# Batches 1 to 3 of a block-sparse attention: three terms of softmax times values summed in one set of PSUM columns

## The chip, the cores and the metric

One core of one Trainium2 chip runs the whole program. The metric is the device time of one execution in microseconds (us); the kernel before took 771.23 us (median of three runs, 769.91 to 771.23). The engines are named as in the profile: PE is the matrix engine and PEld its weight loads, DVE is VectorE, ACT ScalarE, POOL GpSimd, and SP the queue that issues most of the DMAs.

## The reference

The input is q, k and v of 4 batches, 8 heads, 768 rows and 64 columns, and three random block numbers for each of 24 blocks of 32 rows. A row block sees its neighbours, the first and the last block, and its three sampled blocks; the first and the last row block see everything. The result goes through a gated feed-forward layer.

```python
scores = scale * np.matmul(q, k.transpose(0, 1, 3, 2))
scores = np.where(mask, scores, -1000000000.0)
attn = np.exp(scores - np.max(scores, axis=-1, keepdims=True))
attn = attn / (np.sum(attn, axis=-1, keepdims=True) + 1e-09)
x = np.matmul(attn, v)                  # heads side by side: 3072 x 512
g, val = x @ w_gate, x @ w_val          # 512 x 1536 each
out = (g * (1.0 / (1.0 + np.exp(-g))) * val) @ w_out
```

## The kernel before

The 3072 rows are cut into 24 tiles of 128 rows (4 row blocks of 32), and these into 9 chunks: three of two tiles (batch 0), then six of three tiles. Each chunk passes through attention and then through the feed-forward layer. From chunk 3 on, and in the feed-forward part of chunk 2, numbers that need more than 16 bits are kept as two fp16 parts, high and low, and a product is the sum of three: high times high, high times low, low times high.

**A row block in batches 1 to 3** is the function `block`; there are 66 of them, worked on in 33 pairs. Its 256 keys are gathered into `kring` and its 256 values into a part of `w2all` (high and low parts side by side, `vg`). `scores` makes the scores on PE (L1157), `top` masks them and takes the maxima on DVE (L1171), `power` exponentiates on ACT (L1189), `high` (ACT, L410) and `low` (DVE, L413) split the result into `pp`, and a DMA transposes `pp` into `pts`. `product` (L1224) multiplies `pts` by the values into a PSUM bank `pv` that the two blocks of a pair share. When both are there, `x_sum` (L1240, DVE) adds the two column parts of each result, from PSUM into SBUF (the space of `pts` is used again), `x_scale` (L1243, DVE) multiplies by the reciprocals `rr` of the softmax sums, `x_turn` (L1249, PE) transposes into the first half of the `pv` bank, and `x_put` writes the feed-forward input `xall` (ACT L1519, DVE L1520).

In `product` four row tiles u stand in four column strips of PE, 32 columns each, and work side by side; four matmuls, one for each strip, are called a quad here. For each of two head groups g there are four quads: the high weights multiply 128 columns (high and low values, `w_ = 2`), the low weights 64 (high values, `w_ = 1`). So a block has 32 matmuls, half of them of 128 columns and half of 64, and 512 columns of a bank hold a pair: 4 results of 64 columns, each in two parts.

**Batch 0** has a form of its own, `pair0`, in fp32: `product` (L1448), then `scaled` (L1456, DVE), which multiplies a PSUM tile of 128 x 256 by `rr`, then a transposition (L1465). Full rows have `full_rows` (L940, L1011). The feed-forward part is `ffn_in` (L1743 in fp32 for chunks 0 and 1, L1749 in fp16 from chunk 2 on; DVE L1758 and L1763; POOL L1771) and `ffn_out` (L1812). The weights come as fp64 and are decoded on DVE by three passes for each pair of rows (L450, L451, L452), up to about 140 us, then split into halves (L410, L413).

**What sets the order.** Every step is a task of one engine, added by `add` with its needs and buffers. `Plan.order` emits the tasks in the order of the list `TURN`, written out by hand: 2750 numbers. Each engine runs its own instructions in that order. The estimates in the calls of `add` (such as `PV_US`) are not read when the program is built; `TURN` alone decides. PSUM has rings of two banks for `qk`, two for `pv` and four for `ffn`.

Of the kernel before, what the change touches and what calls it, by code (L numbers as in the profile page):

```python
# [13 lines left out]
ALU = mybir.AluOpType  # L14
AX = mybir.AxisListType

P = 128
B, H, S, D = 4, 8, 768, 64
BLK = 32
# [16 lines left out]
PV_US = 0.47  # L36
# [154 lines left out]
]  # L191


# [1717 lines left out]
```

## Time and profile before

| | us |
|---|---|
| three timed runs: median (lowest, highest) | 771.23 (769.91, 771.23) |
| the profiled execution | 768.49 |
| its span, first to last instruction | 766.7 |
| PE busy / DVE busy / ACT busy / POOL busy | 736.3 / 568.3 / 481.9 / 239.1 |
| PE without work from 200 to 690 us | 8.1 |

The profiled execution is 2.74 us (0.36%) shorter than the median; outside its span lie 1.8 us. "Busy" of PE counts a matmul from its start to its modelled end, so matmuls that overlap count once. A number behind "x" is a count of instructions. Idle time in brackets is that of the engine just before the row, with what ended it.

### The profile page before, as it was taken

Reading aid. Unit: us, or ns where it says so; the run is one execution under the profiler, and the core shown is the slowest. Engines: PE = TensorE matmul, PEld = TensorE weight load, DVE = VectorE, ACT = ScalarE, POOL = GpSimd, SP = SyncE. Lnnn points to the kernel's source line nnn. Section 1 sums busy time; section 2 is a strip of 40 time slices with the busy share of each in tenths; the row PEclk is TensorE's granted clock in tenths of the full one; section 3 lists DMA queues with packets and bytes.
Section 4 is the critical chain, followed back from the end, with each engine's and each line's share of the span. In section 5 each row is a group of like instructions: output and inputs, shape, how many; then the busy total and the mean of one; then the engine's idle time right before and its main releaser. Section 6 shows DMA issues by size and latency. Waiting matters only on the chain.

```text
span 766.7 us, 22166 instructions
## 1 busy us (share of the span) xinstructions
PE 736.3 (96%) x8793; PEld 467.1 (61%) x8793; DVE 568.3 (74%) x1581; ACT 481.9 (63%) x1117; POOL 239.1 (31%) x290
## 2 busy tenths in 40 slices
PE   4899999999999999999999999999999999999998
PEld 3576888764686556545655465545665566555655
DVE  6999999998899997537999777656977766733220
ACT  4999745886986875855968665755856553443221
POOL 4887012213154322321233232202333332202120
PEclk9999999999999999999999999999999999999999
DMA  8756576467686987887687996886686656350001
GB/s 282 251 182 211 188 239 250 150 209 166 127 180 176 211 159 139 209 266 189 148 195 153 231 187 176 174 168 148 149 144 124 190 109 146 73 98 15 1 1 42
DMA packets 156472, 123.75 MB, mean 161 GB/s; under 512 B 113456, under 2 KB 124080, under 8 KB 156368
## 3 DMA queue, kind: packets, MB, share of 16 engines
q1 hardware_dynamic: 150736, 105.03, 56.5%
q0 software_dynamic: 5632, 17.31, 8.4%
q8 instruction: 69, 1.13, 0.6%
q14 instruction: 35, 0.29, 0.1%
HBM read 84.55 MB, written 11.01 MB: 125 GB/s over the span
## 4 chain that ended last, share of the span: by engine, by line
PE 58%; DVE 26%; ACT 6%; issue 5%; DMA 2%; POOL 1%; DVEq 1%; SPq 0%; POOLq 0%; ACTq 0%
PE p L1749 29%; PE po L1812 20%; PE qk L1157 2%; PE pv L1224 2%; DVE act L1758 2%; DVE act L1763 2%; DVE w1t L413 1%; DMA ptsf<-ppf 1%; DVE pp L413 1%; DVE e L1171 1%; DVE w1t L451 1%; DVE pts L1240 1%; DVE kring L1135 1%; DVE w2all L451 1%; DVE pts L1243 1%
## 5 line engine op out<-in xcount | busy, mean ns | idle before, releaser
L1749 PE MATMUL p<-xall,w1t 128*128 128x384 f16 (+1 forms) x2016 | 323.2, 319 | 1.0 <-DVE act L1758 1.0
L1749 PEld LDWEIGHTS <-w1t 128*128 128x128 f16 x2016 | 194.3, 98 | 115.9 <-issue 4.7
L1771 POOL TENSOR_TENSOR h<-act,h 128x384 f16<-128x384 f32 (+1 forms) x108 | 101.5, 942 | 341.5 <-ACT h L1768 336.6
L1812 PE MATMUL po<-w2all,h 128*128 128x512 f16 (+1 forms) x900 | 191.9, 371 | 0.0
L1812 PEld LDWEIGHTS <-h 128*128 128x128 f16 x900 | 86.6, 98 | 94.4 <-issue 1.9
L1145 POOL DMA_INDIRECT w2all<-vd,vidx x66 | 65.7, 996 | 85.9 <-PE pv L1224 61.7
L1743 PE MATMUL p<-xall,w1t 128*128 128x256 f32 x384 | 87.8, 383 | 1.8 <-DVE act L1758 1.6
L1758 DVE SCALAR_TENSOR_TENSOR act<-act,p 128x384 f32<-128x384 f32 (+1 forms) x108 | 54.0, 503 | 45.9 <-ACT act L1754 43.7
L1768 ACT CAST h<-act 128x384 f16<-128x384 f32 (+1 forms) x108 | 50.5, 471 | 55.5 <-DVE act L1763 55.2
L1754 ACT ACTIVATE act<-p,gsc 128x384 f32<-128x384 f32 (+1 forms) x84 | 47.0, 559 | 53.5 <-PE p L1749 37.5
L1743 PEld LDWEIGHTS p<-xall,w1t 128*128 128x128 f32 x384 | 71.0, 190 | 14.5 <-DVE act L1758 3.1
L1189 ACT ACTIVATE e<-e,nb,es 128x256 f32<-128x256 f32 x132 | 78.2, 593 | 2.2
L413 DVE SCALAR_TENSOR_TENSOR pp<-e,pp 128x512 f16<-128x512 f32 x66 | 49.2, 751 | 14.2 <-ACT pp L410 13.4
L1763 DVE SCALAR_TENSOR_TENSOR act<-act,hs,p 128x384 f32<-128x384 f32 (+1 forms) x84 | 49.4, 590 | 8.8 <-PE p L1749 5.7
L1171 DVE CUSTOM_DVE_ANT_1 e<-qk,msk 128x256 f32<-128x256 f32 x132 | 49.6, 416 | 3.9 <-PE qk L1157 3.4
L410 ACT ACTIVATE pp<-e 128x512 f16<-128x512 f32 x66 | 40.4, 622 | 0.7
L1687 POOL TENSOR_TENSOR sqx<-sqx 128x768 bf16<-128x768 bf16 (+3 forms) x18 | 21.6, 1202 | 60.8 <-ACT sqx L1683 46.6
L1644 ACT ACTIVATE ot<-po,oc 128x512 f32<-128x512 f32 (+1 forms) x25 | 16.6, 664 | 37.6 <-PE po L1812 32.1
L1135 DVE COPY kring<-kst 128x256 f16 x198 | 37.5, 244 | 1.5 <-DMA kst<-stage 0.9
L1157 PE MATMUL qk<-kring,qs 128*32 128x256 f16 x1056 | 35.7, 273 | 0.4
L1186 ACT ACTIVATE nb<-mx,es 128x2 f32<-128x2 f32 x66 | 19.1, 290 | 25.8 <-DVE mx L1171 25.8
L1224 PEld LDWEIGHTS <-pts 128*32 128x32 f16 x2112 | 25.5, 97 | 9.5 <-issue 8.3
(200 smaller groups left out, 980.3 us busy)
## 6 DMA issues: line engine op xcount, KB each, us to landing
stage<-in_w_dram SPq DMA_DIRECT2D x36, 512.0 KB, 5.1
w2all<-vd SPq DMA_DIRECT2D x66, 192.0 KB, 4.1
qraw<-in_q_dram SPq DMA_DIRECT2D x18, 512.0 KB, 4.9
out_dram<-ot SPq DMA_DIRECT2D x19, 256.0 KB, 4.0
qn<-in_q_dram SPq DMA_DIRECT2D x36, 128.0 KB, 3.5
stage<-in_v_dram SPq DMA_DIRECT2D x9, 512.0 KB, 5.6
vd<-stage SPq DMA_DIRECT2D x9, 512.0 KB, 2.8
stage<-in_k_dram SPq DMA_DIRECT2D x9, 512.0 KB, 5.7
```

The source lines that it names most:

```text
L413: nc.vector.scalar_tensor_tensor(lo, src, scale, hi, op0=ALU.mult, op1=ALU.subtract)
L1145: nc.gpsimd.indirect_dma_start(vf[0:96, 1, :], None, bt.vd, bass.IndirectOffsetOnAxis(ap=vidx[0:96, qb : qb + 1], axis=0))
L1157: nc.tensor.matmul(stv[u * BLK : (u + 1) * BLK, g].rearrange("p s k -> p (s k)"), o.q[:, l, u, g, col : col + BLK], kg[:, 2 * u + g].rearr ...
L1171: nc.vector.tensor_tensor_reduce(ev[:, g], stv[:, g], o.g.msk[:, qb, :].unsqueeze(2).broadcast_to([P, 8, BLK]), scale=1.0, scalar=-3.0e38, ...
L1189: nc.scalar.activation(ev[:, g], ev[:, g], AF.Exp, bias=nb_[:, g : g + 1], scale=o.g.es[:, 0:1], accum_out=both["rs"][:, n % 2, g : g + 1],)
L1743: nc.tensor.matmul(t[:, 0:tc_], w[:, i + 1, k_ * P : (k_ + 1) * P], x_k(k_), start=k_ == 0, stop=k_ == NKT - 1)
L1749: nc.tensor.matmul(t[:, 0:tc_], w_[:, f, m, k_, :], x_k(k_, l), start=i == 0, stop=i == 11)
L1758: nc.vector.scalar_tensor_tensor(a_, a_, 1.0, pg.tile[:, 0:tc_], op0=ALU.add, op1=ALU.mult)
L1763: nc.vector.scalar_tensor_tensor(a_, a_, sc, pw.tile[:, 0:tc_], op0=ALU.mult, op1=ALU.mult)
L1768: nc.scalar.copy(hv(f)[:, 0, :], act.tile[:, 0:tc_])
L1771: nc.gpsimd.tensor_tensor(hv(f)[:, 1, :], act.tile[:, 0:tc_], hv(f)[:, 0, :], op=ALU.subtract)
L1812: nc.tensor.matmul(po.tile[:, cs], hv(f)[:, l, ts_], w2h[:, f, m, cs], start=f == 0 and i == 0, stop=f == NF - 1 and i == 2)
```

## The change

In `product` of batches 1 to 3 all three terms go into the same 64 columns: for each group g six quads of 64 columns (for each half cc of the keys: high by high, high by low, low by high) take the place of two of 128 and two of 64. So a block has 48 matmuls and 48 weight loads where it had 32 and 32, over as many columns in all (12 quads of 64 for 4 of 128 and 4 of 64). A pair fills 256 columns of the bank instead of 512. `x_sum` is gone, and `x_scale` reads PSUM where it read SBUF. `TURN` is a new list of 2717 numbers, 33 fewer. DMA work is as before.

```diff
-PV_US = 0.47
+PV_US = 0.48
...
 TURN = [
-    0, 60, 2, 1, 5, 7, 6, 22, 21, 29, 28, 3, 36, 38, 4, 8, 23, 42, 10, 9, 84, 220, 18, 40, 11, 30, 16, 129, 19, 14,
+    0, 60, 2, 1, 5, 7, 6, 22, 21, 29, 28, 3, 36, 38, 4, 8, 42, 23, 10, 9, 84, 220, 18, 40, 16, 11, 129, 17, 19, 30,
...
-            to = pv.tile.rearrange("p (b g l d) -> p b g l d", b=2, g=2, l=2)[:, n % 2]
+            to = pv.tile[:, 0:256].rearrange("p (b g d) -> p b g d", b=2, g=2)[:, n % 2]
 
             for g in range(2):
-                for i, (cc, l) in enumerate(((0, 0), (0, 1), (1, 1), (1, 0))):
+                for i, (cc, l, m) in enumerate((cc, l, m) for cc in range(2) for l, m in ((0, 0), (0, 1), (1, 0))):
                     for u in range(4):
-                        rows_, w_ = slice(u * BLK, (u + 1) * BLK), 1 if l else 2
                         nc.tensor.matmul(
-                            to[rows_, g, 0:w_],
+                            to[u * BLK : (u + 1) * BLK, g],
                             pq[:, g, l, cc, u],
-                            vg[:, cc, 0:w_, 2 * u + g, :],
+                            vg[:, cc, m, 2 * u + g, :],
                             start=i == 0,
-                            stop=i == 3,
+                            stop=i == 5,
                             tile_position=(0, u * BLK),
                         )
...
-        def x_sum():
-            two = pv.tile.rearrange("p (n l d) -> p n l d", l=2, d=D)
-            nc.vector.tensor_reduce(xs(), two.rearrange("p n l d -> p n d l"), axis=AX.X, op=ALU.add)
-
         def x_scale():
             nc.vector.tensor_tensor(
-                xs(), xs(), both["rr"].rearrange("p b g -> p (b g)").unsqueeze(2).broadcast_to([P, 4, D]), op=ALU.mult
+                xs(), pv.tile[:, 0:256].rearrange("p (n d) -> p n d", d=D), both["rr"].rearrange("p b g -> p (b g)").unsqueeze(2).broadcast_to([P, 4, D]), op=ALU.mult
             )
...
-            a = add("DVE", 0.6, x_sum, [a], rank, use=[pv, pts])
-            a = add("DVE", 0.33, x_scale, [a, both["inv"]], rank, use=[pts])
+            a = add("DVE", 0.34, x_scale, [a, both["inv"]], rank, use=[pv, pts])
             a = add("PE", 0.25, x_turn, [a, t_id], rank, use=[pv, pts])
```

The new list leaves the first 83 tasks of PE, the first 121 of DVE and the first 107 of ACT where they were, which reaches to about 90 us; behind that, tasks of all engines stand earlier or later by a few places. Line numbers of the kernel after are 2 to 8 lower. Two places follow.

The first is PE between 103 and 149 us, the time in which it multiplies chunks 0 and 1 by the fp32 weights (`p`, L1743 before, L1735 after). `xs_21` is the last result of chunk 2, the first input of the fp16 feed-forward part, and the row that reads it is its transposition. Before:

```order
L1743 MATMUL p_11_2273<-xall,w1t 128x256 x4
L1743 MATMUL p_11_2291<-xall,w1t 128x256 x4
L1743 MATMUL p_7_2301<-xall,w1t 128x256 x4
L1465 MATMUL pv_21_2013<-ident,xs_21_2287 128x128 x2
L407 LDWEIGHTS ones_h
L407 MATMUL nrm_v_2319<-vacc_2289,ones_h 128x3
L1743 MATMUL p_7_2322<-xall,w1t 128x256 x4
```

After:

```order
L1735 MATMUL p_2_2030<-xall,w1t 128x256 x4
L1735 MATMUL p_2_2050<-xall,w1t 128x256 x4
L1735 MATMUL p_3_2062<-xall,w1t 128x256 x4
L1457 MATMUL pv_21_1974<-ident,xs_21_2067 128x128 x2
L1735 MATMUL p_3_2073<-xall,w1t 128x256 x4
L1735 MATMUL p_4_2085<-xall,w1t 128x256 x4
```

The transposition stood behind 39 of the 48 `p` products of chunks 0 and 1, and now stands behind 21 of them.

DVE makes `xs_21` for it (L1456 before, L1448 after). The same place on DVE, before:

```order
L1574 TENSOR_TENSOR rsf_1_1_1739<-rsf_1_1_1739 128x1
L1575 TENSOR_SCALAR rsf_1_1_1739<-rsf_1_1_1739,vs_921 128x1
L1576 RECIPROCAL rsf_1_1_1739<-rsf_1_1_1739 128x1
L1456 TENSOR_TENSOR xs_21_2287<-pv_21_2013,rr_21_1889 128x256
L413 SCALAR_TENSOR_TENSOR w2all<-w2all,oss 128x512
```

After:

```order
L448 TENSOR_SCALAR w1t<-stage 128x1024
L449 SCALAR_TENSOR_TENSOR w1t<-stage,w1t 128x1024
L1448 TENSOR_TENSOR xs_21_2067<-pv_21_1974,rr_21_2045 128x256
L450 SCALAR_TENSOR_TENSOR w1t<-stage,w1t 128x1024
L1750 SCALAR_TENSOR_TENSOR act_2_2059<-act_2_2059,p_2_2030 128x256
```

It stood behind the last decoding pass, and now stands between the second and the third pass of the last pair of rows of w_gate and w_val (L449 and L450 there are L451 and L452 of the kernel before).

The second place is DVE at the seventh pair of batch 2, where the result of a pair is summed and scaled. Before:

```order
L808 RECIPROCAL rr_14_7905<-rs_13_7378 128x4
L413 SCALAR_TENSOR_TENSOR pp_17_7888<-e_17_7852,pp_17_7888 128x2x256
L1240 TENSOR_REDUCE pts_14_7752<-pv_13_7773 128x256
L1243 TENSOR_TENSOR pts_14_7752<-pts_14_7752,rr_14_7905 128x256
L1171 ISA e_19_8047,mx_19_8048<-qk_19_7944,msk_6146 128x256
```

After:

```order
L805 TENSOR_SCALAR rs_17_8398<-rs_17_8398 128x4
L806 RECIPROCAL rr_18_8702<-rs_17_8398 128x4
L1236 TENSOR_TENSOR pts_14_8372<-pv_13_8259,rr_14_8152 128x256
L1755 SCALAR_TENSOR_TENSOR act_1_8546<-act_1_8546,hs_8460,p_1_8687 128x384
L411 SCALAR_TENSOR_TENSOR pp_18_8710<-e_18_8391,pp_18_8710 128x2x256
```

Two instructions have become one, which reads `pv` itself, and the reciprocals `rr_14` that it needs stand farther ahead of it.

## Rows read from the trace of the kernel before

**Rows 1.** The page, first part: busy time and share of the span, instructions.

```profile
PE 736.3 (96%) x8793; PEld 467.1 (61%) x8793; DVE 568.3 (74%) x1581; ACT 481.9 (63%) x1117; POOL 239.1 (31%) x290
```

**Rows 2.** Four stretches: each engine's busy time; last the clock, DMA share, GB/s.

```profile
core 0: us, PE busy (x) PEld busy (x) DVE busy (x) ACT busy (x) POOL busy (x), PEclk, DMA share, GB/s
0.00:80.00 80.00, 63.85 (x1271) 46.62 (x1273) 70.23 (x175) 66.53 (x175) 56.05 (x105) 0.96 0.69 224
80.00:200.00 120.00, 117.53 (x816) 86.27 (x811) 112.16 (x250) 82.40 (x172) 25.24 (x26) 1.00 0.64 201
200.00:690.00 490.00, 481.94 (x6271) 290.70 (x6270) 370.60 (x1126) 315.42 (x741) 144.35 (x145) 1.00 0.75 164
```

**Rows 3.** Waits of PE from 200 to 690 us: total us, times, longest.

```profile
PE pv L1249 <- DVE pts L1243: 4.4, 7, 1.7
PE pvf L1011 <- DMA ptsf<-ppf: 1.8, 3, 1.2
PE p L1749 <- DVE act L1758: 1.0, 2, 0.8
```

**Rows 4.** The same view of PE, 80 to 200 us.

```profile
PE p L1743 <- DVE act L1758: 1.6, 3, 1.0
PE nrm_k L407 <- ACT stage L417: 0.5, 1, 0.5
PE nrm_w L407 <- ACT wsq L417: 0.4, 1, 0.4
```

**Rows 5.** Three DVE lines: count, shortest, median, longest duration in ns, start times, form.

```profile
L1240 DVE TENSOR_REDUCE pts<-pv x33: 658/683/693, 211.2 to 688.5; 128x256 f32<-128x512 f32 x33
...
L1243 DVE TENSOR_TENSOR pts<-pts,rr x33: 411/425/2392, 212.9 to 689.2; 128x256 f32<-128x256 f32 x33
...
L1456 DVE TENSOR_TENSOR xs<-pv,rr x11: 401/415/425, 29.8 to 144.9; 128x256 f32<-128x256 f32 x11
```

**Rows 6.** DVE by line and form: busy us, mean ns of one.

```profile
L1240 DVE TENSOR_REDUCE pts<-pv 128x256 f32<-128x512 f32 x33 | 22.5, 683 | 10.3 <-PE pv L1224 10.2
L1243 DVE TENSOR_TENSOR pts<-pts,rr 128x256 f32<-128x256 f32 x33 | 20.2, 615 | 1.3 <-issue 0.7
```

**Rows 7.** Timeline at 438 us, DVE, then POOL, then PE: start, duration.

```profile
437.96 0.69 DVE L1240 TENSOR_REDUCE pts<-pv 128x256 f32<-128x512 f32 x1 [1.49 <-PE pv L1224]
438.69 2.39 DVE L1243 TENSOR_TENSOR pts<-pts,rr 128x256 f32<-128x256 f32 x1
...
439.14 2.71 POOL L1687 TENSOR_TENSOR sqx<-sqx 128x768 bf16<-128x768 bf16 x2
...
438.60 0.85 PE L1224 MATMUL pv<-w2all,pts 128*32 128x128 f16 x64
441.13 0.44 PE L1249 MATMUL pv<-ident,pts 128*128 128x128 f32 x2 [1.68 <-DVE pts L1243]
```

**Rows 8.** PE timeline at 204 and 208 us: `product` of one block, then of two.

```profile
204.05 0.51 PE L1224 MATMUL pv<-w2all,pts 128*32 128x128 f16 x32
204.50 4.10 PE L1749 MATMUL p<-xall,w1t 128*128 128x256 f16 x36
208.53 0.86 PE L1224 MATMUL pv<-w2all,pts 128*32 128x128 f16 x64
209.22 1.53 PE L1157 MATMUL qk<-kring,qs 128*32 128x256 f16 x32
```

**Rows 9.** PE by form inside 208.59 to 208.65 us, its second and third quad.

```profile
L1224 PE MATMUL pv<-w2all,pts 128*32 128x128 f16 x4 | 0.2, 230 | 0.0
L1224 PE MATMUL pv<-w2all,pts 128*32 128x64 f16 x8 | 0.2, 193 | 0.0
```

**Rows 10.** DVE, then PE, around 114 us: last decoding triple; `p` products, 8 matmuls each.

```profile
112.98 0.69 DVE L450 TENSOR_SCALAR w1t<-stage 128x1024 int32<-128x1024 int32 x1
113.70 1.23 DVE L451 SCALAR_TENSOR_TENSOR w1t<-stage,w1t 128x1024 int32<-128x1024 int32 x1
114.96 1.23 DVE L452 SCALAR_TENSOR_TENSOR w1t<-stage,w1t 128x1024 int32<-128x1024 int32 x1
...
110.79 5.45 PE L1743 MATMUL p<-xall,w1t 128*128 128x256 f32 x24
```

280 rows, old and new, of the table TURN are left out of this document.

## The prediction

> **What bounds the kernel now.** I read the busy times first: PE works 96% of the span, the next engine, DVE, 74% [rows 1]. Such a share is a mean over stages, so the second view is the four stretches [rows 2]. Before 80 us PE lacks 16.2 of 80 us, but the new list leaves the tasks there in place. From 80 to 200 us PE lacks 120 - 117.5 = 2.5 us, from 200 to 690 us 490 - 481.9 = 8.1 us, and its granted clock is 1.00 of the 2.4 GHz level. So from 80 us on the end is set by how much PE has to do, plus its few waits; 22 us of DVE time are worth only what they take out of those waits. The third view names them. From 200 to 690 us PE waited 4.4 us, in 7 waits, for `x_scale` (L1243) before a transposition, 1.8 us for transposed weights of full rows, and 1.0 us for DVE in the feed-forward part; the rest are pieces of 0.2 us and less [rows 3]. From 80 to 200 us it was 1.6 us for DVE and 0.9 us for ACT [rows 4]. ACT and POOL are never what PE waits for in the second stretch.
>
> **Why `x_scale` is waited for.** Its median is 425 ns and its longest 2392 [rows 5]; the mean is 615 [rows 6], so 33 x (615 - 415) = 6.6 us are stretch. At 438.69 us it took 2.39 us while POOL ran two additions from SBUF to SBUF, and PE stood 1.68 us in front of the transposition behind it [rows 7]: one stretched `x_scale` is more than a third of the 4.4 us. L1456, the same multiplication with the same form but with its large input in PSUM, took at most 425 ns in 11 runs, in the stage in which POOL is busiest (56 of 80 us) [rows 5, 2]. After the change `x_scale` is of this kind. The Trainium skill ("SBUF — State Buffer", Who interferes with whom) has a rule for it: a DVE instruction with two inputs in SBUF contends with a GpSimd instruction that reads SBUF and may block until that ends, one with at most one such input doesn't. The trace agrees (2392 ns against 425 ns); by the rule no order of tasks can bring the stretch back, so the whole 4.4 us would be safe from this cause.
>
> **The change part by part.** The sum is made against the profiled execution, 768.49 us, and then moved to the median.
>
> *The waits behind `x_scale`.* Removed: 33 `x_sum` of 683 ns (22.5 us of DVE) and the 6.6 us of stretch. The shortest way from the last matmul of a pair to its transposition was 0.07 (437.96 us in rows 7 follows the matmuls at once) + 0.68 + 0.43 + 0.06 = 1.2 us and becomes 0.07 + 0.42 + 0.06 = 0.55 us. In the new list the least work that PE has between the two is one pair of `scores` and one `product`, over 1.2 us; elsewhere it is 1.9 us and more. So nothing but DVE's own queue can delay a transposition. Bounds: 0 (DVE is late for other reasons at seven new places) to -4.4 us. I take -4.0, near the end that the row of L1456 speaks for.
>
> *Other waits for DVE from 200 to 690 us* (1.0 us [rows 3]): DVE has 29 us less to do of 370.6 [rows 2]. Bounds -1.0 and 0; I take -0.4.
>
> *The matmuls of `product`.* Alone, one block holds PE 0.45 us, of two in a row each 0.345 (208.53 to 209.22) [rows 8]; the 0.1 is the change between 32 and 128 column strips, paid once a group before and after. In 208.59 to 208.65 us eight matmuls of 64 columns started, beside four of 128 still under way [rows 9]: two quads in 60 ns, 30 ns each. The four quads of 128 then have (345 - 4 x 30) / 4 = 56 ns. A block after is 12 quads of 64: 12 x 30 = 360 ns at most by this row, 12 x 28 = 336 ns if a quad of half the columns takes half of 56. So -9 to +15 ns for a block, times 66: -0.6 to +1.0 us. No row shows more than two such quads in a row, so I take +0.5. The 66 blocks have 1056 more matmuls and 1056 more weight loads; a load of 32 columns lies under the quad ahead of it, as in rows 9. If it doesn't, that is the first rival.
>
> The Trainium skill ("TensorE: Matmul & The Clock Gate", Back-to-back issue gap) speaks against this edit: it gives matmuls of up to 64 columns a floor of about 25 ns from start to start. By it 48 of them would take 1.2 us for a block, an estimate of +0.855 x 66 = +56 us. The trace differs: eight started within 60 ns [rows 9], and 32 took 345 ns [rows 8], so four strips share that floor or it doesn't hold here.
>
> *Stage 80 to 200 us.* The transposition of `xs_21` now stands behind 21 `p` products. In the trace the row of 24 matmuls (three products) that starts at 110.79 holds the 20th to 22nd, so the 21st ends at 110.79 + 2/3 x 5.45 = 114.4 us [rows 10]. On DVE its input now stands behind the second pass of the last decoding triple of w_gate and w_val, which ends where the third begins, at 114.96 [rows 10]; plus 0.42 and 0.06 it is there at 115.4. So PE waits 1.0 us where it did not. What waits behind it on PE are the rest of the `p` products; DVE catches up meanwhile, which shortens the waits for L1758 that follow (1.6 us [rows 4]); I take -0.3 of those, +0.7 in all. Bounds: all 2.5 us of waits gone and none added, -2.5; a DVE one triple later (0.72 + 1.26 + 1.23 = 3.2 us more), +4.2.
>
> *At nothing:* the DMAs, whose number is unchanged; POOL's gathers and SP's value loads, which wait for the end of `product` as before (it moves by 15 ns at most); `x_scale`'s new need of the reciprocal, which stands on the same engine ahead of it; the list moved past SP's weight loads, which land ahead of decoding. Each is hidden by the cover of several us that PE has between `scores` and `product`; were it gone, a DMA wait as in rows 3 (0.6 us each) would be the price.
>
> Sum: -4.0 - 0.4 + 0.5 + 0.7 = -3.2, so 768.49 goes to 765.3 and the median 771.23 to **768.0 us**. A difference under 0.2% (1.54 us: 769.7 to 772.8) can't be told from no change.
>
> **The rivals.**
>
> *Short quads don't keep up (slower).* Place: L1224, 66 blocks. If PE starts instructions no faster than the mean over a block of before, 64 in 345 ns, 5.4 ns each, then 96 take 517 ns: +172 ns x 66 = +11.4 us in place of +0.5, and 771.23 - 3.7 + 11.4 = 778.9 us. It decides from 34 ns for a quad on: 4 ns x 12 x 66 = 3.2 us eats the gain. For it: no row shows more than 16 instructions at the faster pace. Against it: those 16 took 60 ns [rows 9], 3.8 ns each, and the slower mean has a cause of its own, the streaming of 128 columns.
>
> *The waits only move (no change).* The new list moved tasks of all engines from 90 us on. If DVE comes one triple later to `xs_21` (+4.2 in place of +0.7), the sum is +0.3: 771.5 us. The same comes out if seven transpositions wait as long for DVE's queue as they did for `x_scale`. For it: DVE is busy 112 of 120 us there [rows 2]. Against it: after 200 us DVE has 119 us free and gets 29 more.
>
> *More than the waits of `x_scale` go (faster still).* With every wait for DVE of rows 3 and 4 gone, quads at 28 ns and no wait at `xs_21`: -4.4 - 1.0 - 0.6 - 1.6 = -7.6, 763.6 us. For it: the 29 us of DVE; against it: the 1.0 us at `xs_21`, worked out from rows.
>
> **How the numbers follow.** Forecast 0.56, waits only move 0.24, short quads 0.12, more goes 0.08. Of the forecast's 0.56 some 0.05 lie inside 0.2%: faster 0.51 + 0.08 = 0.59; same 0.05 + 0.20 = 0.25; slower 0.12 + 0.04 = 0.16, the 0.04 from a list that waits longer than it did. The range reaches from the bound below, 763.5, to the sum of the upper bounds without the first rival, 0 + 0 + 1.0 + 4.2 = +5.2, cut to 775.0, since all bounds seldom meet; the first rival and the tails, under 0.2, stay outside.
>
> **What would show it.** Right: the longest `x_scale` stays under 450 ns; the wait of L1249's successor for `x_scale` falls from 4.4 us under 1 us; two blocks of `product` in a row take 0.67 to 0.72 us; PE is without work under 5 us from 200 to 690 us; one wait of about 1 us stands near 115 us before the transposition of `xs_21`. Wrong: two blocks take over 0.8 us (first rival), or PE lacks 8 us or more after 200 us with waits for other lines (second rival).

## The result, and the profile after

The changed kernel took 777.04 us (median of five runs, 776.57 to 780.03) beside 771.23 us: a ratio of 1.0086, 95% interval 1.0065 to 1.0107, slower by 0.9%. The forecast was 768.0 us. The profiled execution took 777.04 us (span 775.2) beside 768.49 (766.7). Chips differ: in the runs below the kernel before took 769 to 771 us on three of them and 776.5 us on one, so every ratio is taken to runs of before on the same chip.

The page's first part and the stretches of [rows 1, 2], for the kernel after:

```profile
PE 739.5 (95%) x9849; PEld 474.4 (61%) x9849; DVE 543.6 (70%) x1548; ACT 480.8 (62%) x1117; POOL 235.8 (30%) x290
```

```profile
0.00:80.00 80.00, 60.45 (x1179) 43.57 (x1180) 69.39 (x168) 62.74 (x163) 56.71 (x104) 0.94 0.68 220
80.00:200.00 120.00, 118.06 (x858) 87.25 (x857) 109.26 (x236) 80.11 (x169) 25.98 (x28) 1.00 0.61 190
200.00:690.00 490.00, 479.31 (x7240) 295.76 (x7237) 348.73 (x1112) 319.97 (x755) 139.75 (x145) 1.00 0.78 167
```

`product` alone (L1224 before, L1221 after), PE's busy time from 200 to 700 us, first before, then after:

```profile
200.00:700.00 500.00, 30.23 (x2112) 25.53 (x2112) 1.00 0.74 162
```

```profile
200.00:700.00 500.00, 36.25 (x3168) 32.70 (x3168) 1.00 0.77 165
```

The span grew by 8.5 us, and these rows say where. DVE has 24.7 us less to do, as meant, and the end came later nonetheless.

| PE, us | before | after | difference |
|---|---|---|---|
| without work, 0 to 80 us | 16.15 | 19.55 | +3.4 |
| without work, 80 to 200 us | 2.47 | 1.94 | -0.5 |
| without work, 200 to 690 us | 8.06 | 10.69 | +2.6 |
| without work, rest of the span | 3.7 | 3.6 | -0.1 |
| busy in `product` | 30.2 | 36.2 | +6.0 |
| busy in all else | 706.1 | 703.3 | -2.8 |

Matmuls of `product` overlap their neighbours. Counted from each start to the next one on PE, without waits, `product` takes 25.6 us before and 31.1 after: +5.4 us.

**The waits.** PE's waits from 200 to 690 us, the view of [rows 3], and DVE's `x_scale` (L1236), the view of [rows 5]:

```profile
PE pv L1242 <- DVE pts L1236: 1.6, 2, 0.8
PE nrm_v L405 <- ACT stage L415: 1.5, 1, 1.5
PE pv L1221 <- DMA pts<-pp: 1.3, 1, 1.3
PE pv L1221 <- issue: 1.3, 1, 1.3
PE xn L1683 <- DVE mx L1169: 1.0, 1, 1.0
PE pv L1221 <- DMA w2all<-vd: 1.0, 1, 1.0
PE p L1741 <- issue: 0.9, 1, 0.9
PE qk L1155 <- DVE kring L1134: 0.9, 2, 0.5
PE pv L1221 <- DVE rsf L968: 0.7, 1, 0.7
```

```profile
L1236 DVE TENSOR_TENSOR pts<-pv,rr x33: 392/418/426, 214.7 to 691.3; 128x256 f32<-128x256 f32 x33
```

`x_scale` is never stretched (426 ns at most, 2392 before), and PE waits 1.6 us for it in place of 4.4. But four waits of 1.0 to 1.5 us that [rows 3] don't have stand beside it, and 2.2 us are called "issue": PE waited for nothing that the profile shows.

**The early stretch.** Each engine's instructions and waits are the same, one for one, until past 80 us, and yet this stretch lost most of PE's time without work. Around 20 us, DVE before, POOL before, then after: the three copies of DVE (shortest, median, longest in ns, start times), POOL and PE:

```profile
20.29 3.18 DVE L630 COPY w2all<-w2all 32x1536 f32<-32x1536 f32 x3
```

```profile
20.14 1.22 POOL L1340 COPY w1t<-kst 128x128 f32 x3
22.16 0.77 POOL L1340 COPY w1t<-kst 128x128 f32 x3 [0.79 <-PE qk L1388]
```

```profile
L628 DVE COPY w2all<-w2all x3: 690/1217/5555, 19.4 to 26.2; 32x1536 f32<-32x1536 f32 x2, 32x1024 f32<-32x1024 f32 x1
```

```profile
19.23 0.95 POOL L1339 COPY w1t<-kst 128x384 f32<-128x384 f32 x2
20.12 2.88 POOL L1332 COPY w1t<-kst 128x128 f32 x12
22.96 0.95 POOL L1339 COPY w1t<-kst 128x384 f32<-128x384 f32 x2
```

```profile
23.01 0.43 PE L1440 MATMUL pv<-w2all,pts 128*32 128x64 f32 x16
27.69 0.55 PE L1440 MATMUL pv<-w2all,pts 128*32 128x64 f32 x12 [4.25 <-DVE pts L1425]
```

Before, three copies of DVE took 3.18 us in all. After, the first alone took 5.55 us: it began at 19.42 us beside a row of POOL copies without a gap, which ended at 22.96 + 0.95 = 23.91 us, and it ended 1.07 us later, at 24.98. PE stood 4.25 us for the copy of `pts` queued behind it, and its granted clock in the first 80 us fell from 0.96 to 0.94. The Trainium skill ("SBUF — State Buffer", Who interferes with whom) says that a copy on DVE can take both of its SBUF ports and then shares one pair with GpSimd, and that the second to come is blocked until the first finishes. The trace agrees on the block, but the copy waited for the whole row of copies of 283 and 497 ns, not for one. In the kernel before it was POOL that waited at this place: the second of the three copies in its row at 20.14 us took 747 ns beside the copy of DVE, where others take 283.

**The blocks of `product`.** PE's timeline, two blocks in a row (the form of [rows 8], third row):

```profile
402.87 0.98 PE L1221 MATMUL pv<-w2all,pts 128*32 128x64 f16 x96
403.66 0.29 PE L1155 MATMUL qk<-kring,qs 128*32 128x256 f16 x3
```

0.79 us from start to next line where before had 0.69. By the starts of single matmuls in this row the first ten quads follow each other at 29 to 30 ns (39 at the very first) and the rest at 32 to 35, with steps of 37 and 55. The four matmuls of a quad start some 3 ns apart at first; in the rest the matmuls come evenly, most of them 8 to 9 ns apart. Over all blocks ahead of `scores`, the time from the first start to the next line is 351 ns before and 367 after for one block (medians, 12 runs each), 691 and 804 for two (8 and 6), 1030 and 1301 for three (1 and 2).

### The profile page after: what moved, and what is told of

The parts are those of the page before. It is cut to its first block, busy times and chain, and to the rows that moved or that the text cites. A ratio compares the mean times of both kernels' runs of the same rounds, so it can differ in the third digit from the quotient of the medians.

```text
span 775.2 us, 24252 instructions
## 1 busy us (share of the span) xinstructions
PE 739.5 (95%) x9849; PEld 474.4 (61%) x9849; DVE 543.6 (70%) x1548; ACT 480.8 (62%) x1117; POOL 235.8 (30%) x290
## 5 line engine op out<-in xcount | busy, mean ns | idle before, releaser
L1763 POOL TENSOR_TENSOR h<-act,h 128x384 f16<-128x384 f32 (+1 forms) x108 | 98.3, 915 | 344.5 <-ACT h L1760 330.8
L1143 POOL DMA_INDIRECT w2all<-vd,vidx x66 | 63.9, 967 | 91.0 <-PE pv L1221 63.4
L1735 PE MATMUL p<-xall,w1t 128*128 128x256 f32 x384 | 87.5, 383 | 1.1 <-DVE act L1750 0.9
L1735 PEld LDWEIGHTS p<-xall,w1t 128*128 128x128 f32 x384 | 71.1, 190 | 13.1 <-DVE act L1750 2.0
L1221 PEld LDWEIGHTS <-pts 128*32 128x32 f16 x3168 | 32.7, 95 | 13.7 <-issue 11.6
L1221 PE MATMUL pv<-w2all,pts 128*32 128x64 f16 x3168 | 36.2, 196 | 4.6 <-DMA pts<-pp 1.3
```

The source lines that it names most:

```text
L1143: nc.gpsimd.indirect_dma_start(vf[0:96, 1, :], None, bt.vd, bass.IndirectOffsetOnAxis(ap=vidx[0:96, qb : qb + 1], axis=0))
L1221: nc.tensor.matmul(to[u * BLK : (u + 1) * BLK, g], pq[:, g, l, cc, u], vg[:, cc, m, 2 * u + g, :], start=i == 0, stop=i == 5, tile_positio ...
L1735: nc.tensor.matmul(t[:, 0:tc_], w[:, i + 1, k_ * P : (k_ + 1) * P], x_k(k_), start=k_ == 0, stop=k_ == NKT - 1)
L1763: nc.gpsimd.tensor_tensor(hv(f)[:, 1, :], act.tile[:, 0:tc_], hv(f)[:, 0, :], op=ALU.subtract)
```

## The experiments

My theory was now: the price is the number of PE's instructions in `product`, and the early stall is a second loss. Rivals: the new list costs it; or the 64-column layout does. All runs, with the time beside before on the same chip:

| run | instructions a block | longest copy of `load_v0` on DVE, us | ratio (95%) |
|---|---|---|---|
| after | 96 | 5.56 | 1.0086 (1.0065 to 1.0107) |
| after_again | 96 | 5.57 | 1.0078 (1.0052 to 1.0104) |
| edit_old_list | 96 | 6.72 | 1.0045 (1.0025 to 1.0066) |
| old_edit_new_list | 64 | 1.22 | 1.0080 (1.0051 to 1.0109) |
| spread_reduce | 96 | 1.74 (a sum) | 1.0036 (1.0015 to 1.0057) |
| three_products | 64 | 1.30 | 0.9998 (0.9983 to 1.0013) |
| before_reduce | 64 | 1.74 (a sum) | 1.0015 (1.0003 to 1.0026) |
| edit_old_list_reduce | 96 | 1.74 (a sum) | 1.0078 (1.0061 to 1.0094) |
| half_columns | 96 | 1.74 (a sum) | one run, 789.7 beside 776.5 us |
| old_split | 96 | 5.96 | 1.0108 (1.0081 to 1.0135) |
| two_terms | 64 | 1.74 (a sum) | 0.9941 (0.9918 to 0.9964) |
| pool_later | 64 | 1.34 | 0.9978 (0.9960 to 0.9996) |
| late_split | 64, last 32 blocks 96 | 5.57 | 1.0073 (1.0044 to 1.0102) |

**The changed kernel once more** (no edit).

> The changed kernel, unaltered. Its first profile shows a copy on DVE (L628, 32x1536) that took 5.56 us at 19.4 us, behind a row of copies on POOL, where the same copy took 1.21 us in the profile of before, although the lists of DVE, POOL, ACT and PE are the same up to there. If this is chance, the copy takes 1.2 to 1.3 us in this profile and the time lies 3 to 4 us under 777.0 in some executions. If the program fixes it, the copy takes 5 us or more again and the time is 776.5 to 777.5.

Measured: 775.82 us (772.80 to 780.29). In this second profile of the same program the copy took 5572 ns, after 5555: the stall belongs to the program, it isn't chance from run to run. PE's waits at 269, 274, 293 and 330 us come back 3 us later, at 272, 277, 296 and 333. The stage from 80 to 200 us does not repeat so well: PE has 4.3 us without work there, where the first profile had 1.9.

**The edit in the old order, and the old code in the new order.** The first is the changed kernel with the list of before (its 33 `x_sum` taken out), the second the kernel before with the list of after:

```diff
 TURN = [
-    0, 60, 2, 1, 5, 7, 6, 22, 21, 29, 28, 3, 36, 38, 4, 8, 42, 23, 10, 9, 84, 220, 18, 40, 16, 11, 129, 17, 19, 30,
+    0, 60, 2, 1, 5, 7, 6, 22, 21, 29, 28, 3, 36, 38, 4, 8, 23, 42, 10, 9, 84, 220, 18, 40, 11, 30, 16, 129, 19, 14,
...
```

> The new product and the new x_scale in the order of the kernel before (its list without the 33 x_sum, the rest in the same order). Theory of the quads: 66 blocks cost about 75 ns more each in either order, +5.0 us, the waits behind x_scale go, -2.8 us, so 773 to 774 without the early stall and 777 to 778 with it. Rival, the new list is what costs: 767.5 to 769, as predicted for the edit, with two blocks in a row still near 0.8 us but with fewer waits elsewhere.

> The old product, x_sum and x_scale in the order of the changed kernel (each x_sum directly ahead of its x_scale). If the new list is what costs, 775 or more. If the list is innocent, 770 to 772.5, as before: the waits behind x_scale stay (4 us) and the product stays at 0.69 us for two blocks. If the early stall belongs to the list, the copy L630 at 19 to 20 us takes over 5 us here too and the time is 774 to 776.

Measured: 774.60 us (770.45 to 777.01, 12 runs) and 776.94 us (771.93 to 779.54, 9 runs), beside 770.33. The waits of PE from 200 to 690 us, edit in the old order, then old code in the new order:

```profile
PE qk L1149 <- issue: 4.0, 2, 2.8
PE pv L1215 <- DMA pts<-pp: 1.2, 1, 1.2
PE pv L1215 <- issue: 0.5, 2, 0.4
PE p L1735 <- DVE act L1744: 0.2, 1, 0.2
```

```profile
PE pv L1243 <- DVE pts L1237: 4.8, 4, 1.9
PE pv L1218 <- DMA pts<-pp: 3.1, 1, 3.1
...
PE qk L1151 <- DVE kring L1130: 1.3, 2, 0.8
PE nrm_v L401 <- ACT stage L411: 1.2, 1, 1.2
PE xn L1685 <- DVE mx L1165: 1.0, 1, 1.0
PE pv L1218 <- DVE rsf L964: 0.9, 1, 0.9
```

So the edit loses in either order. With the old list it takes away nearly every wait for another engine's data (from the 7.2 us of [rows 3] to 1.4); what is left is "issue". The waits of `nrm_v` for ACT's `stage`, of `xn` for DVE's `mx`, and those for `rsf` and `kring` stand in both kernels with the new list and in neither with the old one: they come with the list. With the old code, which has 22 us more for DVE, that list costs 0.8% by itself. Whether it costs the changed kernel time is unclear: 1.0045 and 1.0078 have overlapping intervals.

**The early stall taken away.** The three copies as sums over an axis of length 1, in the changed kernel, in the kernel before and in the edit with the old list:

```diff
-            copy(to, src.unsqueeze(1).broadcast_to(list(to.shape)))
+            if copy == nc.vector.tensor_copy:
+                nc.vector.tensor_reduce(to, src.unsqueeze(1).broadcast_to(list(to.shape)).unsqueeze(3), axis=AX.X, op=ALU.add)
+            else:
+                copy(to, src.unsqueeze(1).broadcast_to(list(to.shape)))
```

> The changed kernel, with the three copies of load_v0 that stand on DVE (L628) written as a sum over an axis of length 1, which the runs so far never show stretched beside POOL (the sums of x_sum took 658 to 693 ns in 33 runs). Theory of the early stall: the 5.56 us copy becomes 1.6 to 1.8 us, PE is without work about 16 instead of 19.6 us before 80 us, and the time falls by 3 to 4 us to 773 to 774. Rival, the early stall is absorbed by later waits or isn't in the timed runs: 776.5 to 777.5.

> The kernel before, with the three copies of load_v0 as sums over an axis of length 1. In its profile these copies were not stretched (1.21 us). If the sum alone had a merit, or moved other things, the time would fall here too, to 768 or less; if it only keeps POOL from stopping the copy, there is nothing to win and the three sums cost DVE 1.6 us more before the first product: 770 to 772.

> New product and x_scale in the order of the kernel before, and the three copies of load_v0 as sums. By the pieces measured so far: product +5.4 us, waits after 200 us -1.5, other -0.5 to -2, no early stall: 771 to 772.5 beside 770.3, that is 2.5 to 3.5 us under the same kernel with the copies (774.6). Rival, the stall at 19 us isn't what this order loses: 774 or more.

Measured: 773.04 us (769.63 to 778.70), 777.17 (775.54 to 778.51) and 781.89 (781.13 to 783.00), the last two on the chip on which before took 776.52. The sums in the changed kernel:

```profile
L629 DVE TENSOR_REDUCE w2all<-w2all x3: 1216/1732/1744, 18.4 to 22.3; 32x1536 f32<-32x1536 f32 x2, 32x1024 f32<-32x1024 f32 x1
```

The changed kernel wins 2.8 us (775.82 to 773.04; the intervals of the two ratios just overlap), the kernel before nothing: so the stall is worth about 3 us there. PE's time without work before 80 us fell less than expected, to 17.9 us and not to 16: it is 16.2 to 18.6 us in the nine profiles without the stall and 19.4 to 19.7 in the five with it, so of the 3.4 us in the table above 1 to 3 are the stall's. The third run missed its expectation of 771 to 772.5 on a chip of 770.3: on its own chip it lost 5.4 us, a ratio of 1.0078 where the same kernel with the copies had 1.0045 on another chip, so what the stall costs is seen in one kernel only. Its waits from 200 to 690 us:

```profile
PE qk L1152 <- issue: 5.3, 13, 0.6
PE pv L1218 <- issue: 3.8, 8, 0.5
```

9.1 us of "issue" in 21 pieces, where three_products, with 64 instructions a block, has 5.3 us on that chip (rows below) and before_reduce 5.0.

**The waits behind `x_scale` by themselves.** The kernel before, with `x_sum` and `x_scale` as three instructions, none of which has two large inputs in SBUF:

```diff
 def x_sum():
-    nc.vector.tensor_reduce(xs(), two.rearrange("p n l d -> p n d l"), axis=AX.X, op=ALU.add)
+    nc.vector.tensor_tensor(two[:, :, 1], two[:, :, 1], rr_all(), op=ALU.mult)
+    nc.vector.tensor_tensor(xs(), two[:, :, 0], rr_all(), op=ALU.mult)
...
 def x_scale():
-    nc.vector.tensor_tensor(xs(), xs(), rr_all(), op=ALU.mult)
+    nc.vector.tensor_tensor(xs(), two[:, :, 1], xs(), op=ALU.add)
```

> The kernel before with its old product and list, but x_sum and x_scale are replaced by three multiplications or additions that each read one large tensor from PSUM and at most one from SBUF: column part 2 times the reciprocal in place in PSUM, column part 1 times the reciprocal to SBUF, then the two added (three x_sum stand a few DVE tasks later, since they now need the reciprocal). Prices the waits behind x_scale alone. Theory that the stretch comes from two inputs in SBUF beside POOL: each of the three takes 410 to 430 ns, none over 500, PE's wait for the last of them falls from 4.4 us to under 2, and with 5 us more of unstretched DVE work the time is 766.5 to 769 beside 770.3. Rival, the waits come from DVE's queue and not from the stretch: the waits stay at 4 us or more and the time is 770 to 773.

Measured: 776.18 us (774.35 to 779.50) beside 776.52. The last of the three; PE's waits; then the transposition of [rows 7] on PE in before_reduce, which has the old `x_scale` on the same chip, and here:

```profile
L1241 DVE TENSOR_TENSOR pts<-pv,pts x33: 392/424/425, 214.5 to 696.1; 128x256 f32<-128x256 f32 x33
```

```profile
PE pv L1217 <- issue: 3.5, 8, 0.6
PE p L1745 <- DVE act L1754: 2.7, 3, 1.2
PE qk L1150 <- issue: 1.8, 5, 0.5
PE pv L1245 <- DVE pts L1241: 1.6, 4, 0.7
```

```profile
445.73 0.44 PE L1252 MATMUL pv<-ident,pts 128*128 128x128 f32 x2 [0.93 <-DVE pts L1246]
```

```profile
444.10 0.44 PE L1245 MATMUL pv<-ident,pts 128*128 128x128 f32 x2
```

The stretch is gone, and with it PE's wait at the place of [rows 7]: the cause of that wait is shown. What the stretch costs in all is not. The 4.4 us of [rows 3] are from another chip; on this one before_reduce, with an `x_scale` of up to 2385 ns, waits 1.6 us behind it in all, as much as three_products, and the time doesn't move.

**Half of the columns.** In five of the six quads of a group 32 columns in place of 64, in the kernel of spread_reduce:

```diff
-                            to[u * BLK : (u + 1) * BLK, g],
+                            to[u * BLK : (u + 1) * BLK, g, 0 : 32 if i else 64],
...
-                            vg[:, cc, m, 2 * u + g, :],
+                            vg[:, cc, m, 2 * u + g, 0 : 32 if i else 64],
```

> The changed kernel with the sums, in which of the six products of a group only the first has its 64 columns, the five others the first 32 (so half of the values lack all terms but the first). The number of matmuls and weight loads is unchanged. Theory that the quads are limited by the supply of instructions: after the first seven to eleven a quad takes 33 to 34 ns as before, with the same steps of 47 and 57 ns, and the 66 blocks fall by less than 2 us in all. Rival, streaming of the columns: quads of 32 columns take 15 to 17 ns throughout and the blocks fall by 8 us or more. Rival, weight loads that are not hidden: quads at 28 to 30 ns from the first on, and no faster.

Measured, PE's timeline at the two blocks shown above for after:

```profile
401.97 0.97 PE L1224 MATMUL pv<-w2all,pts 128*32 128x64 f16 x96
402.76 0.29 PE L1158 MATMUL qk<-kring,qs 128*32 128x256 f16 x3
```

0.79 us again, with little over half of the columns. By the single starts the quads of 32 columns come at 25 ns at first, four of them, and then at 33 to 36, as those of 64 do: the time that they saved was waited for. For one block ahead of `scores` the median is 367 ns in both kernels. So neither columns nor unhidden weight loads (which would slow the first quads too) set the length of a block, but the rate at which PE hands out instructions: 33 to 34 ns for the eight of a quad, 4.2 ns each. The weight loads show where it sets in: they start in fours up to the 33rd or 34th load of a row of blocks and from there on evenly, 8 to 9 ns apart, in 39 of the 45 rows of after and in 35 of 45 here. The matmuls follow some quads later, mostly after 8 to 12 quads of 64 columns (64 to 96 instructions). In every run each matmul has a weight load of its own, so the runs can't tell 4.2 ns for an instruction from 8.4 ns for a weight load. Why this run as a whole is 13 us over before is not shown. Its "issue" waits are 7.4 us before `product` alone. In one of them, at 273.5 us (0.52 us), the DMA view of 273.3 to 274.1 us shows an instruction packet under way:

```profile
q8 instruction: 1, 0.02, 10.5%
```

Of this run's 32 idle pieces of over 0.1 us between 200 and 690 us, 11 (5.3 of 17.1 us) overlap such a packet, which are under way 12% of the time. With the packets shifted by up to 60 us against the idle pieces it would be 6 on average, so this is a hint and no cause.

**The number of instructions alone.** The kernel before, each matmul of 64 columns written as two of 32: same columns, same `x_sum`, same list, 96 instructions a block:

```diff
-                for i, (cc, l) in enumerate(((0, 0), (0, 1), (1, 1), (1, 0))):
+                for i, (cc, l, h) in enumerate(((0, 0, 0), (0, 1, 0), (0, 1, 1), (1, 1, 0), (1, 1, 1), (1, 0, 0))):
...
+                        half = slice(32 * h, 32 * h + 32)
```

and the opposite, the changed kernel (with the sums) with two of the three terms:

```diff
-for l, m in ((0, 0), (0, 1), (1, 0))
+for l, m in ((0, 0), (0, 1))
```

> The kernel before, in which each matmul of 64 columns of product is written as two of 32 columns: a block has the same columns, column parts and x_sum as before, but 96 instructions (48 matmuls, 48 weight loads) in place of 64, as many as in the changed kernel. Theory that the number of instructions is the price of the edit: the product of the 66 blocks rises by 4 to 6 us (single blocks 0.36 us, two in a row 0.76 to 0.83), and the kernel is slower than before by 4 to 8 us, the waits behind x_scale kept. Rival, the price belongs to the 64-column layout of the edit: blocks stay at 0.345 us in a row and the time within 0.2% of before.

> The changed kernel with the sums (L628), without the third term of the product (low weights times high values is left out), so 64 instructions a block in place of 96, all with 64 columns. Theory of the instructions: a block takes 0.23 to 0.26 us (eight quads of 29 to 33 ns), the product falls by 7 to 9 us and the time to 3 to 6 us under before, which is what the rest of the edit and of the list is worth with the early stall gone. Rival, the product isn't where the time went: the time falls by under 4 us beside the changed kernel with the sums (1.0036 of before) and stays at or over before.

Measured: 779.05 us (777.97 to 781.54) and 766.30 us (763.72 to 768.95), beside 770.53. `product`, 200 to 700 us, first the split, then the two terms:

```profile
200.00:700.00 500.00, 37.44 (x3168) 32.91 (x3168) 1.00 0.75 162
```

```profile
200.00:700.00 500.00, 25.70 (x2112) 21.86 (x2112) 1.00 0.77 164
```

The old code with nothing but more instructions is 8.5 us slower, more than the change; `product` grew by 7.2 us, and the early stall is there too. But its price is not the rate of 4.2 ns: its two blocks ahead of `scores` take 885 ns, beyond 2 x 96 x 4.2 = 0.81 us. Its single starts show each quad of 32 columns at 25 to 28 ns, not at half of 29, beside 55 ns for those of 128, and four such quads in place of two of 64 make up the 86 ns by which one block grew (351 to 437); in none of the 20 blocks that stand alone do the loads turn even. So this run shows that cutting a matmul has a price at the same columns; the rate rests on half_columns and on the single starts.

With 64 instructions the changed kernel has 10.3 us less in `product` (36.0 in spread_reduce) and is 0.6% faster than before. But it has a third fewer columns too, and its `product` is 4.5 us below that of before (25.7 beside 30.2), as much as the 4.2 us by which the kernel is faster (770.53 to 766.30). So a gain of the rest of the edit is not shown by it.

**Where the early stall comes from.** First POOL shifted against DVE in the kernel before, by seven iotas; then the split in the last three chunks only:

```diff
+            if o.eng is nc.gpsimd and not idled:
+                idled.extend(nc.gpsimd.iota(idle, pattern=[[0, 32]], base=0, channel_multiplier=1) for _ in range(7))
```

```diff
-                for i, (cc, l, h) in enumerate(((0, 0, 0), (0, 1, 0), (0, 1, 1), (1, 1, 0), (1, 1, 1), (1, 0, 0))):
+                halves = (0, 1) if ci >= 6 else (0,)
+                steps = [(0, 0, 0)] + [(cc, 1, h) for cc in range(2) for h in halves] + [(1, 0, 0)]
```

> The kernel before with seven small iotas on POOL (about 0.7 us) ahead of its first copies of keys, so that these start near 16.9 us, as in the changed kernel, and not at 16.2 us. Theory that the early stall hangs on the phase of POOL and DVE and not on the edit: the first copy of load_v0 on DVE takes over 4 us here too, PE is without work 3 us more before 80 us, and the time is 2 to 4 us over before. Rival, the stall belongs to the edit: the copy takes 1.2 to 1.3 us, as before, and the time is within 0.2% of before.

> The kernel before with the matmuls of 64 columns split in two, as in the run in which every block was split (+8.5 us, of which product +6.9 and waits before 80 us +3.3), but only in the 32 blocks of the last three chunks: 1024 more instructions on PE, all after its 6900th, past 400 us. The price of the instructions: product +3.0 to +3.6 us. Theory that the stall at 19 us goes with the longer program of PE, wherever it was made longer (so far it stands in the four programs with 96 instructions a block that keep the copy, and in none of the four with 64): the copy takes over 5 us, PE waits 3 us more before 80 us, and the time is 5.5 to 7.5 us over before. Rival, the stall is a coincidence of the early phase: 1.2 to 1.4 us for the copy and 2.5 to 4.5 us over before in all.

Measured: 769.10 us (767.13 to 770.32) beside 770.53, which is 0.2% faster with an interval that ends at 0.04%, and 776.07 us (772.52 to 777.11) beside 769.21. The copies, POOL shifted, then the late split; between them POOL's first copies of keys, shifted:

```profile
L632 DVE COPY w2all<-w2all x3: 691/1202/1343, 19.0 to 22.7; 32x1536 f32<-32x1536 f32 x2, 32x1024 f32<-32x1024 f32 x1
```

```profile
17.70 0.76 POOL L1344 COPY w1t<-kst 128x128 f32 x3
```

```profile
L630 DVE COPY w2all<-w2all x3: 690/1216/5565, 19.1 to 25.9; 32x1536 f32<-32x1536 f32 x2, 32x1024 f32<-32x1024 f32 x1
```

This shift of POOL does not bring the stall. It does not settle the theory of the phase, though: the iotas moved POOL's first copies of keys to 17.70 us, not to the 16.9 that was meant. With 1024 more instructions of PE past 400 us the stall is there, at 19 us. So it goes with the length of PE's program (the page's DMA part counts 69 packets of queue q8, instructions, before, 73 here and 77 after), in all four programs of greater length that keep the copies (five profiles) and in none of the four with the old length; on each of two chips both outcomes were seen. How a longer program reaches the first 20 us isn't shown. What goes with the stall in all nine profiles that keep the copies is the moment at which DVE's copy meets POOL's row: 189 to 242 ns after the start of the POOL copy beside it in the five, 63 to 161 ns in the four, where the next POOL copy waits instead (746 to 751 ns in place of 283). No run sets this moment, so the cause stays open. Inside late_split the two forms of `product` stand side by side; two blocks ahead of `scores`, PE's timeline:

```profile
410.63 0.86 PE L1227 MATMUL pv<-w2all,pts 128*32 128x128 f16 x64
411.32 0.94 PE L1157 MATMUL qk<-kring,qs 128*32 128x256 f16 x28
```

```profile
620.82 1.07 PE L1227 MATMUL pv<-w2all,pts 128*32 128x128 f16 x96
621.71 0.30 PE L1157 MATMUL qk<-kring,qs 128*32 128x256 f16 x4
```

0.69 and 0.89 us, in one execution. The two splits do not part the price of all 66 blocks (P) from that of the stall (S): P + S = 8.5 and P x 32/66 + S = 6.9 by the medians give P = 3.2 and S = 5.3, the ratios (8.3 and 5.6 us) P = 5.2 and S = 3.1. The intervals of the two ratios overlap, so neither pair is more than an estimate.

## Why the prediction was wrong

- **The matmuls of `product`, +0.5 us (bounds -0.6 and +1.0): this step failed.** It took 28 to 30 ns a quad from 60 ns of trace [rows 9] and let twelve quads go on so. That holds for the first 8 to 12 quads: one block ahead of `scores` costs 16 ns more, just over the upper bound of 15. Behind them a quad costs 33 to 34 ns with steps up to 57, so two blocks cost 113 ns more, three 271. PE's busy time in `product` rose by 6.0 us (5.4 without overlaps), and some 5 of the 9 us between forecast and result lie here.
- **The first rival** was the right mechanism at about half its size: it feared 5.4 ns an instruction, the runs show 4.2 after the first 64 to 96. Its threshold of 34 ns a quad was met almost to the ns. That its 778.9 us lies near the measured 777.04 is luck: half of its price is there, and the early stretch and other waits make up the rest. It had a chance of 0.12 on the strength of 16 instructions; the old product at 64 x 4.2 = 0.27 us a block never reached the limit, so no row of before could show it.
- **The Trainium skill's floor** ("TensorE: Matmul & The Clock Gate", Back-to-back issue gap) was left open between a floor that the strips share and one that doesn't hold here. Its 25 ns from start to start appear in half_columns and old_split as the distance of two quads of 32 columns, which is the distance inside one column strip; so the traces fit a floor for each strip, which four strips pass side by side. Taken over all matmuls, its +56 us would have been ten times too much.
- **"Before 80 us the new list leaves the tasks there in place"** was right and yet the step failed: PE was without work 3.4 us longer in the same tasks, 1 to 3 of them by the stalled copy. The prediction had no term for a stretch whose instructions don't change.
- **The waits behind `x_scale`, -4.0 us:** the cause of the stretch was right (three_products; 426 ns at most), the wait fell by 2.8 us, in the bounds. The sign that I named, under 1 us, failed with 1.6 (0.8 in after_again). That the time falls with the wait was not shown: three_products, which takes away the stretch alone, is at 0.9998.
- **Other waits, -0.4 us:** wrong. Without those for `x_scale` PE's waits from 200 to 690 us rose from 3.7 to 9.1 us, 2.2 of them "issue", most of the rest with the new list; this is the rival "the waits only move", and its sign (8 us or more without work after 200 us) is met with 10.7, though before had 8.1 already. With the old list the same edit leaves 1.4 us of waits for data.
- **Stage 80 to 200 us, +0.7 us:** the wait ahead of `xs_21` came, 0.3 us at 118.3 us in place of 1.0 at 115; the stage as a whole has 0.5 us less without work in the first profile and 1.8 more in after_again, so its sign is not settled.
- **The range** has a slip of its own: the lower bounds add up to -4.4 - 1.0 - 0.6 - 2.5 = -8.5, which is 762.7 us and not 763.5. The measured time lies beyond the upper end as well before it was cut, 776.4.

## What to carry to other kernels

Count matmuls with their loads, not columns alone, when a matmul is cut into smaller ones: in this kernel a quad on four strips is worth its place while its columns last longer than its four matmuls and four loads take to start (56 ns for 128 columns against 33), and a rate read from 16 of them says nothing on a row of 96. A saving on an engine that isn't the bound does not pay for more work on the engine that is: DVE lost 24.7 us here and PE's `product` gained 6.0. And look at a copy of DVE that starts beside a row of GpSimd copies even where the edit is far from it: whether it is blocked turned here with edits that leave its stretch as it was.

## What the runs showed of the hardware

- PE started the four matmuls and four loads of a quad at 25 to 30 ns, until 56 to 96 instructions had gone, then at 33 to 34 ns: 4.2 ns an instruction, or 8.4 a weight load, for quads of 64 columns as of 32 (367 ns a block with either). The loads turned to this pace after the 33rd or 34th.
- Quads of 32 columns came no closer than 25 ns, those of 64 at 28 to 30, those of 128 at 54 to 56.
- A DVE copy of 32 x 1536 fp32 (1.21 us) waited 4.3 us, to the end of a gapless row of GpSimd copies of 283 and 497 ns; as a sum over one element it took 1.73 us beside the same row. In four profiles the copy was not held up for long (1.20 to 1.30 us), and a GpSimd copy of 283 ns took 746 to 751 ns instead.
- PE's "issue" waits from 200 to 690 us depend on the chip: 5.0 and 5.3 us with 64 instructions a block and 9.1 with 96 on the chip of 776.5 us; on the others none in the profile of before, 2.2 in after and 4.5 in edit_old_list.
